# The first input tile loaded as two partition halves on two queues, and one output tile stored whole

## The chip, the cores and the metric

The kernel runs on one core of a Trainium2 chip. The metric is the device time of one execution in microseconds. The core has engines with instruction queues of their own: TensorE (PE in the profile, with its weight loads as PEld), VectorE (DVE), ScalarE (ACT), GpSimd (POOL) and SyncE (SP). In this kernel SP and ACT issue transfers between memory and the on-chip buffers, each on a queue of its own (SPq and ACTq in the profile), and POOL issues three tiny ones. Sixteen DMA engines carry them all.

## The reference

A block over 2048 tokens of width 448. Its input x is normalised per token; the result xn goes through a state-space layer and through a gated layer, and both are multiplied and added to x:

```python
xn = _layernorm(x, axis=-1)
s = _A_ref(xn, A_Lambda_re, A_Lambda_im, A_B_re, A_B_im, A_C_re, A_C_im, A_log_dt, A_Dskip)
g = _silu(_B_ref(xn, B_w_gate, B_w_up, B_w_down))
return x + s * g
```

The state-space layer is a projection of xn to 448 complex numbers, a recurrence over the tokens, and a projection back:

```python
Bu = jnp.einsum("bld,pd->blp", x + 0j, B_bar)
for t in range(L):
    h = Lam_bar[None, :] * h + Bu[:, t, :]
    hs.append(h)
y = 2.0 * jnp.einsum("blp,dp->bld", hseq, Cmat).real + x * Dskip[None, None, :]
```

The gated layer is `(sigmoid(xn @ w_gate) * (xn @ w_up)) @ w_down`, with 1792 inner columns.

## The kernel before

The tokens are 16 tiles of 128 rows, and four tiles make a chunk of 512 tokens. Tile t lies in `x_all[:, t, :]` with one token per partition. Chunk by chunk the kernel transposes the normalised tiles into `xnT`, multiplies with the gate and up weights `wG` and `wU` (14 blocks of 128 columns per chunk, `gu_mm`, L796 and L797: two 64-row matmuls side by side), projects with B (`b_phase`, L870 to L887), runs the recurrence on VectorE as two real scans in rotated coordinates (`ssm_pair`, `ssm_stack`), and forms the down projection (L1012) and the projection with C (L1041). The last steps of an output tile are on VectorE (L1050 to L1057), and SP stores it from one of three buffers `o_t` (L1061).

The order of the work on each engine is not written out by hand. Every operation is recorded with its engine, an estimated cost, and the keys that it reads and writes. A planner (`Plan.solve`) gives each one a latest start from the needs of TensorE, whose order is fixed, then simulates the engines with these estimates, and `emit` writes the instructions in the order of the simulated starts. The estimate of a transfer goes by its queue, its bytes and a rate, or by a given landing time (`land`). Transfers of SP and ACT take eight completion semaphores in turn; a transfer waits until the one eight places before it has landed. A changed transfer at the head therefore moves the semaphores of all that follow, and can change the order elsewhere.

At the head, what matters is this. SP and ACT first issue the four x tiles of chunk 0 (`load_x`, which calls `load`; the transfer is L357), tile 0 and tile 2 on SP, tile 1 and tile 3 on ACT. Behind them come the first two column blocks of `wG`, one half on each queue and each in two parts (`load_w0`), and then, on SP alone, the rest of `wG`, `wU`, four more x tiles and the row `dbc`, and the transposing loads of B (`b_load`, buffer `bT`, L394). TensorE first runs ten matmuls on constants (`warm_mm`, L443). VectorE computes the statistics of tile 0 (`bn`, L449, and `aggr`, L455), ACT the root (`root`, L483), VectorE the reciprocal (L480) and the normalised tile (`norm`, L516). TensorE transposes it (`pe_transpose`, L555 and L557), ACT copies the result out (L565), and the first gate matmuls run tile by tile (`last_tile`, L814 and L815). The statistics of tile 1 stand on VectorE between those of tile 0 and the norm of tile 0. The part of the B projection that comes first (L873) needs copies that POOL makes from `bT` (L735 and L741).

At the end, `yout` makes one output tile. Which rows one store takes is in `rows`: the tiles of the third chunk (`c == 2`) are stored as two halves of 64 rows, the others whole.

Of the kernel before, what the change touches and what calls it, by code (L numbers as in the profile page):

```python
# [14 lines left out]
ACT = mybir.ActivationFunctionType  # L15
# [3 lines left out]
D = 448  # L19
F = 1792  # L20
P = 128
H = 64
# [28 lines left out]
def dve2(n):  # L51
    return 0.067 + n / 1920.0


def dve1(n):
    return 0.067 + n / 960.0
# [17 lines left out]
class Plan:  # L74
# [10 lines left out]
    def add(self, eng, cost, fn, r=(), w=(), dma=0, lat=None, chain=False, name="", rate=230e3):  # L85
        o = Op()
        o.idx, o.eng, o.cost, o.fn, o.dma, o.name = len(self.ops), eng, cost, fn, dma, name
        o.lat = LAT.get(eng, 0.0) if lat is None else lat
        o.pre, o.suc, o.rate = {}, [], rate
        o.slot, o.land = None, 0.0  # L90
        if dma and eng != "POOL":
            o.slot, self.n_dma = self.n_dma, self.n_dma + 1
        o.start = o.end = None
        for k in r:
            if k in self.w:
                self._edge(self.w[k], o, True)
        for k in w:
            for q in self.r.get(k, ()):
                self._edge(q, o, False)
            if k in self.w:  # L100
                self._edge(self.w[k], o, True)
        for k in w:
            self.w[k] = o
            self.r[k] = []
        for k in r:
            if k not in w:
                self.r.setdefault(k, []).append(o)
        if chain or eng == "PE" or (eng in ("DVE", "ACT") and self.seq):
            key = ("chain", eng)
            if key in self.last_of:  # L110
                self._edge(self.last_of[key], o, None)
            self.last_of[key] = o
        self.ops.append(o)
        return o
# [132 lines left out]
def kernel(  # L247
# [22 lines left out]
    x_src = A_x.rearrange("b (n p) d -> p (b n) d", p=P)  # L270

    def sbt(name, shape, dt=BF16):
        return sb.tile([P] + list(shape), dt, name=name)
# [9 lines left out]
    x_all = sbt("x_all", [NT, D])  # L283
# [67 lines left out]
    add = pl.add  # L351
# [3 lines left out]
    def load(eng, key, nbytes, o, i, cost=0.45, r=(), rate=230e3, land=0.0):  # L355
        e = {"SP": Q, "ACT": A, "POOL": G}[eng]
        add(eng, cost, lambda: e.dma_start(out=o, in_=i), w=[key] if not isinstance(key, list) else key,  # L357
            r=r, dma=nbytes, chain=True, rate=rate).land = land

    def load_x(t0, n, q="SP", r=(), rate=230e3, land=0.0):  # L360
        load(q, [("x", t) for t in range(t0, t0 + n)], n * P * D * 2,
             x_all[:, t0:t0 + n, :], x_src[:, t0:t0 + n, :], r=r, rate=rate, land=land)
# [37 lines left out]

    def load_p(eng, k, r=()):
        load(eng, ("vrow", k), D * 2, vrow[k:k + 1, 0:D], (A_log_dt, A_Lambda_im, A_Lambda_re)[k].unsqueeze(0), cost=0.75, r=r)
    load_x(0, 1, "SP")
    load_x(1, 1, "ACT")
    load_x(2, 1, "SP", rate=180e3)
    load_x(3, 1, "ACT", rate=180e3)
    add("ACT", 0.05, lambda: A.preload_act_table_set("sqrt_and_others"), w=["sqrttab"], lat=1.3, chain=True)
    load_w0("SP", 0, "A", land=5.7)
    load_w0("ACT", 1, "A", land=5.9)
# [127 lines left out]
    def next_acc():  # L537
        a = acc_n[0] % 2
        acc_n[0] += 1
        return a  # L540
# [482 lines left out]
    def yout(c, j, first=False, banks=None, parts=((0, D),)):  # L1023
        js = slice(j * P, j * P + P)
        t = c * TPC + j
        g = gt_of[c, j]
        o = o_n[0] % NO
        o_n[0] += 1
        q = t % NXD
        xq = xd[q][:]  # L1030
        for pi, (c0, c1) in enumerate(parts):
            key, y = banks[pi] if banks else (lambda a: (("acc", a), acc[a][:, 0:D]))(next_acc())
            y = y[:, 0:c1 - c0]

            on_pe = len(parts) > 1 and pi == len(parts) - 1

            def f(y=y, c0=c0, c1=c1, on_pe=on_pe):
                if on_pe:
                    T.matmul(y, lhsT=ident[:, :], rhs=xq[:, c0:c1], start=True, stop=False)
                for i, (hm, cm) in enumerate(K_ORDER):  # L1040
                    T.matmul(y, lhsT=hT[c % 2][:, hm, js], rhs=cT[:, cm, c0:c1],  # L1041
                             start=(i == 0 and not on_pe), stop=(i == 6))
            n = c1 - c0
            add("PE", (8 if on_pe else 7) * (0.004 + n / 2400.0) + (SW if first else 0), f,
                r=cTk + [("hT", c % 2, p) for p in range(4)] + ([("xd", q), "ident"] if on_pe else []),
                w=[key], name=f"y{c}.{j}")
            ok = ("o", o, pi)
            od = o_t[o][:, c0:c1]
            if on_pe:
                add("DVE", dve1(n), lambda od=od, y=y, c0=c0, c1=c1: V.tensor_tensor(out=od, in0=y, in1=g_t[g][:, c0:c1], op=ALU.mult),  # L1050
                    r=[key, ("gt", g)], w=[ok])
            else:
                add("DVE", dve1(n), lambda od=od, y=y, c0=c0, c1=c1: V.tensor_tensor(out=od, in0=y, in1=xq[:, c0:c1], op=ALU.add),  # L1053
                    r=[key, ("xd", q)], w=[ok])
                add("DVE", dve2(n), lambda od=od, c0=c0, c1=c1: V.tensor_tensor(out=od, in0=od, in1=g_t[g][:, c0:c1], op=ALU.mult),
                    r=[ok, ("gt", g)], w=[ok])
            add("DVE", dve2(n), lambda od=od, c0=c0, c1=c1: V.tensor_tensor(out=od, in0=od, in1=x_all[:, t, c0:c1], op=ALU.add),  # L1057
                r=[ok, ("x", t)], w=[ok])
            rows = (0, H, P) if c == 2 else (0, P)
            for r0, r1 in zip(rows, rows[1:]):  # L1060
                add("SP", 0.45, lambda od=od, c0=c0, c1=c1, r0=r0, r1=r1: Q.dma_start(  # L1061
                    out=out_flat[t * P + r0:t * P + r1, c0:c1], in_=od[r0:r1, :]),
                    r=[ok], w=[("store", t, pi, r0)], dma=n * 2 * (r1 - r0))
# [104 lines left out]
    for c in (2, 3):  # L1168
        def mid(banks, c=c):
            for j in range(4):  # L1170
                down(c - 1, j, bank=banks[j])
                yout(c - 2, j)
        for i in range(0, 4):
            gu_step(c, i)
        b_phase(c, mid)
        if c == 2:
            prepare(3)
        for i in range(4, 14):
            gu_step(c, i)
        whole(c)  # L1180

    yout(2, 0, True)
    yout(2, 1)
    free_banks = []
    for s in range(3):
# [50 lines left out]
```

## Time and profile before

| | |
|---|---|
| median of 3 runs | 183.61 us (183.5 to 183.76) |
| profiled execution | 183.83 us, span 182.1 us |
| TensorE busy | 177.9 us of the span |
| VectorE busy | 166.4 us |
| ScalarE busy | 97.0 us |
| GpSimd busy | 40.7 us |
| x tiles of chunk 0, 112 KB each, issue to landing | SP 2.6 us, ACT 2.8 us (medians of two) |
| whole stores of 128 rows, 112 KB, issue to landing | 1.7 us, median of 11 |
| stores of 64 rows, 56 KB, issue to landing | 2.0 us, median of 8 |

The span runs from the first to the last instruction; the profiled execution's own time holds 1.73 us more around it. A row of the timeline gives start and length in microseconds, the engine, the line of the kernel, the operation, its output and inputs, and in brackets the idle time before it and what ended that. Rows of SPq and ACTq are the issuing of transfers by those queues, not the transfers. Matmul ends in the profile are modelled, so the distance between starts is what tells the pace of TensorE. A row of waits gives who waited for whom, the sum, how often, and the longest.

### The profile page before, as it was taken

To read this page: it belongs to the slowest core of one execution; us is meant where nothing else is said; L and a number is where in the kernel's file an instruction comes from. 1 tells how busy PE (TensorE), PEld (TensorE's weight loads), DVE (VectorE), ACT (ScalarE), POOL (GpSimd) and SP (SyncE) were. 2 spreads that over 40 slices of the span, in tenths; PEclk is the share of its full clock that TensorE was granted. 3 is DMA by queue.
4 is the path that set the end of the run, shared out by engine and by line. 5 is a ranking of instruction groups with operands and counts; after the bars stand their busy time and mean duration, and the time that the engine had idled before them with its cause. 6 is when DMAs were issued, how large, how long until landed. Compare 5 with 4: busy or idle time off the path is not lost.

```text
span 182.1 us, 3611 instructions
## 1 busy us (share of the span) xinstructions
PE 177.9 (98%) x1404; PEld 88.4 (49%) x1404; DVE 166.4 (91%) x296; ACT 97.0 (53%) x158; POOL 40.7 (22%) x96
## 2 busy tenths in 40 slices
PE   8999999999999999999999999999999999999992
PEld 2764444564554444445554444444555444455551
DVE  2917999999999999999999999999999999999773
ACT  3699997958899983364145543348110533411100
POOL 7183546700038997000004100000000000000000
PEclk9999999999999999999999999999999999999999
DMA  4999999999100390000004900001000000002221
GB/s 130 251 216 214 203 148 166 265 235 235 51 0 0 72 133 0 0 4 0 0 2 82 148 0 0 4 0 65 10 4 0 25 27 29 0 0 63 58 74 39
DMA packets 30003, 13.44 MB, mean 74 GB/s; under 512 B 19489, under 2 KB 29985, under 8 KB 29985
## 3 DMA queue, kind: packets, MB, share of 16 engines
q1 hardware_dynamic: 29120, 12.74, 34.4%
q10 hardware_dynamic: 768, 0.46, 0.8%
q8 instruction: 11, 0.18, 0.4%
q14 instruction: 8, 0.06, 0.1%
q0 software_dynamic: 96, 0.00, 0.0%
HBM read 6.77 MB, written 1.84 MB: 47 GB/s over the span
## 4 chain that ended last, share of the span: by engine, by line
PE 97%; DVE 1%; issue 0%; DVEq 0%
PE gu L796 43%; PE gu L1012 15%; PE acc L1041 11%; PE acc L1012 9%; PE gu L884 9%; PE gu L443 2%; PE gu L814 2%; PE acc L887 2%; PE gu L870 2%; PE acc L796 1%; PE gu L797 1%; PE acc L555 0%; PE acc L873 0%; PE gu L555 0%; DVE o_t L1057 0%; DVE o_t L1053 0%
## 5 line engine op out<-in xcount | busy, mean ns | idle before, releaser
L796 PE MATMUL gu<-xnT,wU 64*128 64x512 bf16 x196 | 45.8, 376 | 0.0
L797 PE MATMUL gu<-xnT,wU 64*128 64x512 bf16 x196 | 45.8, 376 | 0.0
L796 PE MATMUL gu<-xnT,wG 64*128 64x512 bf16 (+1 forms) x189 | 41.3, 360 | 0.0
L797 PE MATMUL gu<-xnT,wG 64*128 64x512 bf16 (+1 forms) x189 | 41.3, 360 | 0.0
L830 ACT ACTIVATE sig<-gu 128x1024 f32<-128x1024 f32 x21 | 21.4, 1022 | 25.8 <-PE gu L797 21.0
L1012 PEld LDWEIGHTS <-hF 128*128 128x128 bf16 x224 | 21.9, 98 | 20.6
L796 PEld LDWEIGHTS <-wU 64*128 64x128 bf16 x196 | 18.4, 94 | 22.9
L796 PEld LDWEIGHTS <-wG 64*128 64x128 bf16 x196 | 18.4, 94 | 19.9
L1012 PE MATMUL gu<-wd,hF 128*128 128x448 bf16 x140 | 28.0, 352 | 0.0
L833 DVE SCALAR_TENSOR_TENSOR hF<-sig,gu 128x1024 bf16<-128x1024 f32 x21 | 25.3, 1205 | 0.5 <-PE gu L797 0.3
L951 DVE TENSOR_TENSOR_SCAN wv<-c_r,st,z 128x512 bf16<-128x512 f32 x18 | 22.8, 1270 | 0.0
L1041 PE MATMUL acc<-cT,hT 128*128 128x448 bf16 (+1 forms) x112 | 22.6, 346 | 0.0
L1018 ACT ACTIVATE g_t<-gu 128x448 bf16<-128x448 f32 x10 | 5.4, 539 | 27.7 <-PE gu L1012 16.8
L797 PEld LDWEIGHTS <-wU 64*128 64x128 bf16 x196 | 18.4, 94 | 0.0
L797 PEld LDWEIGHTS <-wG 64*128 64x128 bf16 x196 | 18.4, 94 | 0.0
L1012 PE MATMUL acc<-wd,hF 128*128 128x448 bf16 x84 | 16.9, 352 | 0.0
L884 PE MATMUL gu<-xnT,bT 128*128 128x512 bf16 x72 | 16.7, 379 | 0.0
L1041 PEld LDWEIGHTS <-hT 128*128 128x128 bf16 x119 | 11.5, 98 | 10.1 <-issue 0.4
L898 ACT CAST bus<-gu 128x1024 bf16<-128x1024 f32 x12 | 12.0, 1010 | 5.8 <-PE gu L870 5.3
L527 POOL COPY xn<-xn 128x448 bf16<-128x448 bf16 x12 | 8.0, 675 | 29.9 <-ACT xn L521 29.8
L449 DVE BATCH_NORM_STATS2 bst<-x_all 128x6 f32<-128x448 bf16 x12 | 7.0, 611 | 7.7 <-DMA x_all<-in_A_x_dram 7.7
L1053 DVE TENSOR_TENSOR o_t<-acc,xd 128x448 bf16<-128x448 f32 (+1 forms) x16 | 9.5, 597 | 2.7 <-PE acc L1041 2.6
(156 smaller groups left out, 265.6 us busy)
## 6 DMA issues: line engine op xcount, KB each, us to landing
wd<-in_B_w_down_dram SPq DMA_DIRECT2D x2, 784.0 KB, 6.3
out_dram<-o_t SPq DMA_DIRECT2D x11, 112.0 KB, 1.7
wU<-in_B_w_up_dram SPq DMA_DIRECT2D x2, 448.0 KB, 11.2
x_all<-in_A_x_dram SPq DMA_DIRECT2D x2, 448.0 KB, 4.6
wG<-in_B_w_gate_dram SPq DMA_DIRECT2D x2, 336.0 KB, 7.3
wU<-in_B_w_up_dram SPq DMA_DIRECT2D x2, 336.0 KB, 9.4
wG<-in_B_w_gate_dram SPq DMA_DIRECT2D x2, 224.0 KB, 5.6
x_all<-in_A_x_dram SPq DMA_DIRECT2D x2, 224.0 KB, 9.1
```

Source lines behind the costliest of these rows:

```text
L449: add("DVE", 0.56 if t < TPC else 0.6, lambda: V.bn_stats(out=bst[b][:], in_=x_all[:, t, :]), r=[("x", t)] + ([("xnT", 0, 3, "a")] if 3 < ...
L527: add("POOL", 0.25 if n == H else 0.6, lambda: G.tensor_copy(out=o[:, D:D + n], in_=o[:, 0:n]), r=[("xn", b)], w=[("xnw", b)])
L796: T.matmul(bank[0][:, ts], lhsT=w_[0:H, s, ms], rhs=x[0:H, SL[s], ts], start=(s == 0), stop=(s == 6))
L797: T.matmul(bank[1][:, ts], lhsT=w_[H:P, (s + 1) % 7, ms], rhs=x[H:P, SL[s], ts], start=(s == 0), stop=(s == 6))
L830: add("ACT", act(1024), lambda: A.activation(th, gu[a][:], ACT.Tanh, scale=0.5), r=[("gu", a)], w=[tk])
L833: add("DVE", dve1(1024), lambda: V.scalar_tensor_tensor(out=ho, in0=th, scalar=1.0, in1=gu[a][:], op0=ALU.add, op1=ALU.mult), r=[("gu", a) ...
L884: T.matmul(gu[slots[pt]][:, i, :], lhsT=bT[:, kt, i, pt * P:pt * P + P], rhs=x[:, kt, :], start=(first and kt == 0), stop=(not first and k ...
L898: add("ACT", act(1024), lambda: A.copy(out=bus[u][:], in_=gu[slots[pt]][:]), r=key(pt), w=[("bus", u)])
L951: dve(1.194, lambda k=k: V.tensor_tensor_scan(out=wv[:, k, :], data0=rb, data1=z[:, k, :], initial=(st[pt][:, k, :] if c else 0.0), op0=AL ...
L1012: T.matmul(d, lhsT=hF[c % 2][:, m, h, js], rhs=wd[:, ft, :], start=(ft == 0), stop=(ft == FT - 1))
L1041: T.matmul(y, lhsT=hT[c % 2][:, hm, js], rhs=cT[:, cm, c0:c1], start=(i == 0 and not on_pe), stop=(i == 6))
L1053: add("DVE", dve1(n), lambda od=od, y=y, c0=c0, c1=c1: V.tensor_tensor(out=od, in0=y, in1=xq[:, c0:c1], op=ALU.add), r=[key, ("xd", q)], w ...
```

## The change

Tile 0 is loaded as two transfers of 64 partitions, the lower half on SP and the upper half on ACT. An operation without an engine joins both into the key `("x", 0)` that the statistics read. Tile 1 moves from ACT to SP, behind the lower half; tile 2 moves from SP to ACT, behind the upper half; tile 3 moves from ACT to SP, behind tile 1. SP thus issues three x transfers and ACT two. In the stores, the first tile of the third chunk (`j == 0`) is stored whole and the other three as halves, so the number of transfers that take semaphores is the same at the end as before.

```diff
-    load_x(0, 1, "SP")
-    load_x(1, 1, "ACT")
-    load_x(2, 1, "SP", rate=180e3)
-    load_x(3, 1, "ACT", rate=180e3)
+    for h, eng in enumerate(("SP", "ACT")):
+        ps = slice(h * H, h * H + H)
+        load(eng, ("x0", h), H * D * 2, x_all[ps, 0, :], x_src[ps, 0, :])
+    add("NONE", 0.0, lambda: None, r=[("x0", 0), ("x0", 1)], w=[("x", 0)], lat=0.0)
+    load_x(1, 1, "SP")
+    load_x(2, 1, "ACT", rate=180e3)
+    load_x(3, 1, "SP", rate=180e3)
...
-            rows = (0, H, P) if c == 2 else (0, P)
+            rows = (0, H, P) if c == 2 and j else (0, P)
```

The changed kernel has three lines more at its head, so a line number below that is higher by 3 in its profile (L449 becomes L452). In the instruction lists the order on TensorE is the same. On ACT, one evacuation of a gate block (L827) stands ahead of the norm of tile 4 (L521) instead of behind two norms, and one cosine table (L673) ahead of two norms; on POOL a copy of `bT` (L735) stands ahead of the copy of tile 6 (L527) instead of behind it; on VectorE three instructions change places with neighbours. The fourth `load_w0` transfer, on ACT, gets a wait for the semaphore of the lower half of tile 0.

## The prediction

> **What bounds the kernel now.** I read the page first: the share of TensorE, the chain that ended last, and the transfers.
>
> ```profile
> span 182.1 us, 3611 instructions
> PE 177.9 (98%) x1404; PEld 88.4 (49%) x1404; DVE 166.4 (91%) x296; ACT 97.0 (53%) x158; POOL 40.7 (22%) x96
> PE 97%; DVE 1%; issue 0%; DVEq 0%
> out_dram<-o_t SPq DMA_DIRECT2D x8, 56.0 KB, 2.0
> x_all<-in_A_x_dram SPq DMA_DIRECT2D x2, 112.0 KB, 2.6
> ```
>
> TensorE is the whole chain. A change to loads can only count where TensorE waits. I therefore took the list of waits for the whole span next. Only the first three of these rows stop TensorE or feed what stops it.
>
> ```profile
> POOL bT L741 <- DMA bT<-in_A_B_im_dram: 1.0, 1, 1.0
> PEld L555 <- DVE g_t L516: 0.9, 1, 0.9
> PEld L873 <- POOL bT L741: 0.5, 2, 0.3
> ```
>
> There are two places. The first is the start. The timeline of the first microseconds shows it (start, length, instruction):
>
> ```profile
> 0.72 0.87 SPq L357 DMA_DIRECT2D x_all<-in_A_x_dram  x2
> 0.73 0.90 ACTq L357 DMA_DIRECT2D x_all<-in_A_x_dram  x2
> 1.64 4.66 SPq L357 DMA_DIRECT2D wG<-in_B_w_gate_dram  x6
> 1.69 1.61 ACTq L357 DMA_DIRECT2D wG<-in_B_w_gate_dram  x2
> 3.26 0.63 DVE L449 BATCH_NORM_STATS2 bst<-x_all 128x6 f32<-128x448 bf16 x1 [3.26 <-DMA x_all<-in_A_x_dram]
> 4.03 0.59 DVE L449 BATCH_NORM_STATS2 bst<-x_all 128x6 f32<-128x448 bf16 x1
> 4.75 0.38 DVE L516 TENSOR_SCALAR g_t<-x_all,mvf,rsd 128x448 bf16<-128x448 bf16 x1
> 5.19 0.82 PE L555 MATMUL acc<-ident,g_t 128*128 128x128 bf16 x6
> ```
>
> Tile 0 lands at 3.24, its statistics start at once, the normalised tile is ready at 5.13, and the first transposes start at 5.19. The ten warming matmuls are spaced 0.427 us and the last starts at 4.56, so TensorE would be free at 4.99. It loses only 0.20 us to tile 0.
>
> The second place is the first projection with B, at 29 us:
>
> ```profile
> 28.65 0.53 POOL L741 COPY bT<-bT 64x64 bf16<-64x64 bf16 x2 [1.02 <-DMA bT<-in_A_B_im_dram]
> 28.94 0.09 PEld L873 LDWEIGHTS <-bT 64*128 64x128 bf16 x1 [0.32 <-POOL bT L741]
> 29.23 0.09 PEld L873 LDWEIGHTS <-bT 64*128 64x128 bf16 x1 [0.20 <-POOL bT L741]
> ```
>
> Here TensorE waits some 0.27 us for two POOL copies of the last bT transfer, which lands at 28.54. That transfer is the end of one line of transfers that SP issues without a pause from 3.68 us (x, wG, wU, dbc, bT). So two chains meet at 29.2: TensorE's own work, with 0.27 us to spare, and the line of SP's transfers, with nothing to spare. Behind that place TensorE starts every matmul where the one before it ends, apart from a constant 0.09 us at each change between 64-row and 128-row tiles. The table of stretches shows how full the transfers are (the last two columns are DMA share and GB/s):
>
> ```profile
> 2.20:3.40 1.20, 1.20 (x5) 0.42 (x3) 0.14 (x1) 0.74 (x1) 1.12 (x4) 1.00 0.98 334
> 3.40:4.40 1.00, 1.00 (x4) 0.34 (x3) 0.97 (x3) 0.19 (x1) 1.00 (x8) 1.00 0.50 121
> 4.40:5.40 1.00, 1.00 (x5) 0.21 (x4) 0.90 (x6) 0.40 (x2) 0.31 (x4) 1.00 1.03 298
> ```
>
> From 4.4 us the DMA engines are full, and stay so until 22; in 3.4 to 4.4 they are half idle while the first wG blocks start. What is lost there comes out at 29.2.
>
> **The change, part by part.** All is summed against the profiled execution, 183.83 us (span 182.1 and 1.73 around it); the median of the runs shown is 183.61, 0.22 less.
>
> *Tile 0 in halves.* Half the rows per queue means half the packets ahead of the last one. In the trace the sixteen completion packets of tile 0 lie between 2.56 and 2.91, and each of a DMA engine's packets takes 0.041 us. Eight packets of tile 1 run between those of tile 0; without them it ends 8 x 0.041 = 0.33 us earlier. Against it stands the issue. No 64-row load of x is in the trace, but 64-row stores are: eight of them took 0.47 to 0.70 us to issue (mean 0.57) where a 128-row store takes 0.33 to 0.40, and landed 2.0 us after issue where a whole one takes 1.7. So tile 0 lands between 0.33 us earlier and, if the stores' 0.3 us comes whole on top of today's 2.51 us with no packets saved, 0.3 us later. I take the sum of the two effects, 0.33 less 0.2, about 0.1 us earlier. The Trainium skill (DMA: Bandwidth & Descriptors, Anatomy of one DMA) fits 2.0 us plus bytes over 436 GB/s, for the gpsimd path; by it, as an estimate, halving 112 KB saves 0.13 us. The 56 KB stores of this trace contradict the sign, and they are what I go by; with the fit alone the sum would be the no-change case below.
>
> *What an earlier tile 0 is worth.* Statistics, root, reciprocal and norm all follow by the same 0.1 us. Tile 1 moves behind the half on SP: issue at about 0.73 + 0.57 + 0.05 = 1.35, and at tile 2's present 2.59 us to landing it is there at 3.9 instead of 3.41. Its statistics start at 4.03 now, so this is just hidden; its cover is the 0.6 us of tile 0's statistics. TensorE then starts 0.1 us earlier (at most 0.2). Until 6.6 us it runs at half pace (a transpose takes 0.11 us in the chain at 6.01 and 0.06 at 8.30), so this is worth 0.05 to 0.1 us of later work. At 29.2 it is worth nothing, because the bT transfer still lands when it does: 0.
>
> *SP's line.* SP issues three x transfers instead of two before wG: 0.73, plus 0.57, 0.42, 0.42 and 0.05 between them, so wG's first block is issued at 2.29 instead of 1.64 and the second at 3.08 instead of 2.43, ending at 3.69. The third block is issued at 3.68 now, held back by a POOL memset that ends at 3.66 and by tile 1's landing; this 0.64 us of waiting takes up the extra issue almost whole. So from the third block on SP is late by 0 to 0.2 us (0.70 us for the half). On the engines, 64 more rows of x are on SP's queue and 64 fewer on ACT's, and SP's wG packets start up to 0.6 us later in just the half-empty stretch. Before 4.0 us that queue moved only some 27 KB of wG; at 298 GB/s it costs 0.09 us to make up. If the whole ramp shifts by 0.6 us and nothing fills in, 0.6 x 170 GB/s = 100 KB, or 0.33 us. Lower end: ACT's queue, 64 rows lighter, fills the gap, and the line is up to 0.1 us early. I take 0.15 us, nearer the row of what was moved then. It reaches 28.54 unshortened, since SP pauses nowhere, and then TensorE: +0.15 us.
>
> *The new wait on ACT.* Transfers take eight completion semaphores in turn. With one more, the ninth is the second wG block on ACT, which now waits for tile 0's lower half. It is issued at 2.45 now (0.86 us) and lands at 6.89; it would be issued at about 3.2. Behind it on ACT is only the first root at 4.21; ACT is free at 4.06, so this is hidden by 0.15 us. On its queue the block stands behind the first block, whose packets run past 4.6, so most of the 0.75 us is hidden too; TensorE needs it at 7.06. Between 0 and 0.75 - 0.17 = 0.58 us of wait there, of which the 0.27 us at 29.2 takes up all but 0.31. I take 0.
>
> *The store.* Two SP issues (0.56 and 0.59 us) and two transfers become one of some 0.33 us, around 165 us. SP is idle around it and its o_t buffer is needed again three tiles later; TensorE does not wait there: 0. Were the cover gone, it could cost nothing, as it is less work.
>
> *What the planner moves.* The orders on TensorE are the same. ACT evacuates one gate block (0.54 us) ahead of the norm of tile 4, POOL copies bT (0.35 us, after the landing at 24.9) ahead of tile 6's copy (now at 24.07), and on DVE three instructions change places with neighbours. The work that hides them: chunk 1's transposed tiles land at 29.3 to 33.0 and TensorE needs the first at 34.75. A shift of tile 6 by 1.3 us stays inside it. 0.
>
> Sum: 0 + 0.15 + 0 + 0 + 0 = +0.15: 183.98 for the profiled execution, 183.76 against the median; I say 183.8.
>
> **The rivals.**
> 1. *No change, the bT wait hides all.* If the SP line is back on time by the third block (it waits 0.64 us before it now), the start's gain is swallowed at 29.2 and the time stays: 183.6. For it: SP's slack just equals the extra issue. Against: the half-empty engines at 3.4 to 4.4.
> 2. *Faster.* Place: the meeting at 29.2. ACT's lighter queue brings its wG forward, the half-idle stretch is filled better, and the transfer line is early; then TensorE can win up to the 0.27 us that it waits there, no more without a gain at the start as well: 183.61 - 0.27 = 183.34. It decides as soon as bT lands before 28.54. Against: ACT now waits for a landing, and SP has more rows.
> 3. *Slower through SP.* The half costs its whole issue, 0.57 + 0.05 us, because the line is limited by the queue and not by SP's issue: 183.61 + 0.62 = 184.23.
> 4. *Slower through ACT.* The wG block comes 0.75 us late, TensorE stands at 7.06: +0.31, 183.9.
> 5. *The clock.* TensorE's half pace lasts longer than 6.6 us. Each microsecond costs half a microsecond, so 0.74 us later costs 0.37: 184.0 and up. The runs before differ by 0.26 us in all, so this has hardly moved. The Trainium skill (TensorE: Matmul & The Clock Gate, Part 1) says that the window which decides is free-running; no run here shows its phase, and the granted clock reads 1.00 in this stretch although the spacing is double.
>
> **How the numbers follow.** Forecast (0 to +0.35) 0.50; no change 0.20; faster 0.14; through SP 0.09; through ACT 0.05; the clock 0.02. About 0.2%, 0.37 us, is what a measurement can tell from no change. Slower by more: case 3, half of what passes the forecast's upper end (0.04), a part of 4, and 5: 0.17. Faster by more needs both the 0.27 us and the start: 0.07. Within: 0.76. The likeliest case alone spans 183.6 to 183.95; the range takes in most of 2 and half of 3, so 183.35 to 184.2.
>
> **What would show it.** Right: tile 0's statistics start between 3.1 and 3.3, the half loads take 0.45 to 0.7 us to issue, the first transposes start between 5.0 and 5.2, the last bT transfer lands 0.05 to 0.35 us after 28.54, and the wait of L873's counterpart for POOL grows while the rest of TensorE's starts keep their distances. Wrong: bT landing before 28.5 (case 2), a new wait of the 64x128 matmuls on wG at 7 us (case 4), or half pace beyond 7 us (case 5).

## The result and the profile after

The changed kernel takes 184.31 us (median of 16 runs, 183.81 to 184.67). The kernel before takes 183.49 us in the runs beside it (16 runs, 183.33 to 184.48). The ratio is 1.0038, with a 95% interval of 1.0028 to 1.0048. On the 183.61 us that were shown at the start, this is 0.70 us slower (0.51 to 0.88). The forecast was 0.15 us slower, with a range of 183.35 to 184.2: the median lies 0.11 us above the upper end, and its interval (184.12 to 184.49) reaches into the range. A second measurement, told below, gave 1.0033 (1.0018 to 1.0047).

The profiled execution of the changed kernel took 184.67 us (span 182.9), which is the longest of its sixteen. Its waits may therefore be larger than those of a usual execution, and the sizes below go by the medians where both are to be had. Where two values are set side by side, as in 3.12 after 3.26, the first belongs to the kernel in question and the second to the kernel before.

Three lines of the page after: the span, the engines' busy time, and the chain that ended last.

```profile
span 182.9 us, 3605 instructions
PE 177.2 (97%) x1397; PEld 87.8 (48%) x1404; DVE 166.4 (91%) x296; ACT 96.9 (53%) x158; POOL 38.7 (21%) x96
PE 83%; DVE 5%; ACT 4%; DMA 3%; issue 1%; SPq 1%; POOL 1%; DVEq 0%; ACTq 0%
```

TensorE's busy time has not grown (177.2 after 177.9, with seven of 1404 matmuls missing from the records), but the span has, by 0.8 us. The chain was 97% TensorE before; now it also runs through transfers (3%) and VectorE (5%). TensorE waits for others. The waits between 2 and 32 us after say for whom (who waits for whom, sum, times, longest):

```profile
PEld L817 <- DMA wG<-in_B_w_gate_dram: 1.1, 2, 0.7
DVE rsd L502 <- POOL sdb L500: 1.1, 1, 1.1
PE gu L817 <- DMA wG<-in_B_w_gate_dram: 0.8, 2, 0.5
```

None of the three was among the waits before, and the wait for POOL's copies of `bT` is missing. The first microseconds after, as a timeline (start, length, engine, line):

```profile
0.72 1.68 SPq L357 DMA_DIRECT2D x_all<-in_A_x_dram  x3
0.73 1.48 ACTq L357 DMA_DIRECT2D x_all<-in_A_x_dram  x2
2.27 1.47 ACTq L357 DMA_DIRECT2D wG<-in_B_w_gate_dram  x2
2.45 4.25 SPq L357 DMA_DIRECT2D wG<-in_B_w_gate_dram  x6
...
3.12 0.63 DVE L452 BATCH_NORM_STATS2 bst<-x_all 128x6 f32<-128x448 bf16 x1 [3.12 <-DMA x_all<-in_A_x_dram]
4.12 0.63 DVE L452 BATCH_NORM_STATS2 bst<-x_all 128x6 f32<-128x448 bf16 x1 [0.15 <-DMA x_all<-in_A_x_dram]
5.30 0.51 PE L558 MATMUL acc<-ident,g_t 128*128 128x128 bf16 x6
...
7.09 0.23 PE L817 MATMUL gu<-xnT,wG 64*128 64x128 bf16 x1 [0.54 <-DMA wG<-in_B_w_gate_dram]
...
7.83 0.23 PE L817 MATMUL gu<-xnT,wG 64*128 64x128 bf16 x1 [0.23 <-DMA wG<-in_B_w_gate_dram]
```

- Tile 0's statistics start 0.14 us earlier (3.12 after 3.26). Tile 1 lands at 4.09, 0.15 us after VectorE is ready for it, and so the gain is gone: the first transposes start at 5.30 after 5.19.
- SP issues `wG` at 2.45 instead of 1.64, ACT at 2.27 instead of 1.69.
- TensorE stands twice at the first gate matmuls. The first stop ends when SP's first block lands (7.04; it was 5.90). The second ends when SP's second block lands (7.78; it was 6.68). Tile 2's transposes follow at 8.72 after 7.96. **At the head of this execution, 0.76 us are lost.**

What the transfers do meanwhile is seen in the stretches (start and end, length, busy times of the engines; the last two columns are DMA share and GB/s):

```profile
2.20:3.40 1.20, 1.20 (x4) 0.42 (x3) 0.28 (x1) 1.16 (x1) 1.12 (x4) 1.00 0.91 216
3.40:4.40 1.00, 1.00 (x4) 0.32 (x3) 0.81 (x3) 0.42 (x2) 1.00 (x8) 1.00 0.99 293
4.40:5.40 1.00, 0.86 (x4) 0.10 (x3) 0.92 (x5) 0.30 (x1) 0.18 (x4) 1.00 0.82 192
```

In 2.2 to 3.4 the engines move 216 GB/s where they moved 334, which is 142 KB less. The next stretch, half idle before, makes this up (293 after 121). But what it carries is still mostly x, and `wG` comes behind: tiles 1, 2 and 3 land at 4.09, 4.50 and 5.06, where all four tiles had landed by 4.01. In 4.4 to 5.4 the engines move 192 GB/s where they moved 298, so nothing is made up for `wG`.

At 29 us, TensorE and its weight loads after:

```profile
29.71 0.27 PE L876 MATMUL acc<-xnT,bT 64*128 64x256 bf16 x2
29.82 0.92 PE L873 MATMUL gu<-xnT,bT 64*128 64x512 bf16 x4
...
30.35 0.09 PEld L873 LDWEIGHTS <-bT 64*128 64x128 bf16 x1 [0.43 <-issue]
...
30.67 0.50 PE L890 MATMUL acc<-xnT,bT 128*128 128x256 bf16 x3
```

The two 64x256 matmuls, which before stood 0.27 us for POOL, run without a pause: `bT` landed at 27.27, TensorE came 0.76 us later. This gives 0.27 us back. Then TensorE stops again at 30.04, for 0.31 us. The row names no releaser ("issue"). VectorE's reading of a gate bank (L836; the kernel lets TensorE write a bank of matmul results again only when they have been read) ends at 30.29, just before TensorE goes on, so this bank is taken to be what it waits for; in a kernel below the profile names it. The end of this stretch, L890, is 0.79 us late (30.67 after 29.88), and the span ends 0.8 us late. VectorE is late because it was blocked at 22 us, here after:

```profile
22.45 0.73 POOL L500 TENSOR_TENSOR sdb<-veb,halfc 128x2 bf16<-128x2 bf16 x1
23.21 0.17 DVE L502 RECIPROCAL rsd<-sdb 128x2 f32<-128x2 bf16 x1 [1.10 <-POOL sdb L500]
```

and the same reciprocal before, which waited for nothing:

```profile
21.96 0.17 DVE L499 RECIPROCAL rsd<-sdb 128x2 f32<-128x2 bf16 x1
```

POOL's `sdb` for tiles 6 and 7 stands on POOL behind the copy of tile 5, and that copy waits for ACT's norm. On ACT the planner has put the evacuation L830 (L827 before) ahead of the norm of tile 4. The norms come later, then POOL, then VectorE. The cause is argued here from one pair of traces; the experiments with the order test it.

### The profile page after: what moved, and what is told of

Its sections match the earlier page's. It is cut to its first block, busy times and chain, and to the rows that moved or that the text cites. A ratio compares the mean times of both kernels' runs of the same rounds, so it can differ in the third digit from the quotient of the medians.

```text
span 182.9 us, 3605 instructions
## 1 busy us (share of the span) xinstructions
PE 177.2 (97%) x1397; PEld 87.8 (48%) x1404; DVE 166.4 (91%) x296; ACT 96.9 (53%) x158; POOL 38.7 (21%) x96
## 4 chain that ended last, share of the span: by engine, by line
PE 83%; DVE 5%; ACT 4%; DMA 3%; issue 1%; SPq 1%; POOL 1%; DVEq 0%; ACTq 0%
PE gu L799 34%; PE gu L1015 14%; PE acc L1044 11%; PE acc L1015 9%; PE gu L887 8%; ACT hF L833 3%; DVE hF L836 3%; DMA wG<-in_B_w_gate_dram 3%; PE acc L890 2%; PE gu L873 2%; PE gu L817 2%; ACT hT L658 1%; SPq L357 1%; DVE hT L669 1%; PE gu L800 1%
## 5 line engine op out<-in xcount | busy, mean ns | idle before, releaser
L836 DVE SCALAR_TENSOR_TENSOR hF<-sig,gu 128x1024 bf16<-128x1024 f32 x21 | 25.3, 1204 | 0.5 <-PE gu L800 0.3
L887 PE MATMUL gu<-xnT,bT 128*128 128x512 bf16 x65 | 15.3, 379 | 0.4
L530 POOL COPY xn<-xn 128x448 bf16<-128x448 bf16 x12 | 7.5, 627 | 29.8 <-ACT xn L524 29.5
L452 DVE BATCH_NORM_STATS2 bst<-x_all 128x6 f32<-128x448 bf16 x12 | 7.0, 614 | 6.6 <-DMA x_all<-in_A_x_dram 6.6
```

Of the source, the lines that this page charges most:

```text
L452: add("DVE", 0.56 if t < TPC else 0.6, lambda: V.bn_stats(out=bst[b][:], in_=x_all[:, t, :]), r=[("x", t)] + ([("xnT", 0, 3, "a")] if 3 < ...
L530: add("POOL", 0.25 if n == H else 0.6, lambda: G.tensor_copy(out=o[:, D:D + n], in_=o[:, 0:n]), r=[("xn", b)], w=[("xnw", b)])
L836: add("DVE", dve1(1024), lambda: V.scalar_tensor_tensor(out=ho, in0=th, scalar=1.0, in1=gu[a][:], op0=ALU.add, op1=ALU.mult), r=[("gu", a) ...
L887: T.matmul(gu[slots[pt]][:, i, :], lhsT=bT[:, kt, i, pt * P:pt * P + P], rhs=x[:, kt, :], start=(first and kt == 0), stop=(not first and k ...
```

## The experiments

Each kernel was timed against the kernel before on the same chip. The first four shared one chip (before 183.79 us), the next four another (183.78 us), and the last two ran on the first again (183.78 us). Single executions of one kernel spread over 0.5 to 1.7 us, so a trace shows where a wait is, and the ratio with its interval shows what a part costs.

### The head alone, without the new store

```diff
-            rows = (0, H, P) if c == 2 and j else (0, P)
+            rows = (0, H, P) if c == 2 else (0, P)
```

> The head of the changed kernel, with the third chunk's first tile stored in halves as before. Two theories. W: the time is lost because SP issues its first two wG blocks later (2.46 and 3.17 us instead of 1.64 and 2.43), so that they land after TensorE is ready for them; the store has no part in it: +0.5 to +0.9 us against before, the same as the changed kernel. S: a part of the loss is the store and the places of the completion semaphores at the end: less than +0.4 us.

Measured: 184.97 us, ratio 1.0057 (1.0035 to 1.0079). The loss is there without the store. TensorE waits 0.56 us for SP's second `wG` block (landed at 7.68). The interval overlaps that of the whole change. The median is 0.59 us above the one that the change had on this chip (184.38, below), more than the store by itself accounts for (also below); why is not known.

### Tile 3 on SP, no halves

```diff
-    load_x(3, 1, "ACT", rate=180e3)
+    load_x(3, 1, "SP", rate=180e3)
```

(on the kernel before)

> No halves: before, with tile 3 alone moved from ACT to SP, behind tile 2. W: SP's first wG block is issued at about 2.1 us instead of 1.64, TensorE waits for it, and the kernel is 0.2 to 0.6 us slower than before. H, the rival by which the halves themselves cost the time (issue of 64 rows, later tile 1, a normalised tile 0 that is 0.1 us late): tile 0 and tile 1 are loaded as before, so within 0.1 us of before.

Measured: 184.0 us, ratio 0.9997 (0.9979 to 1.0016). SP issues `wG` at 2.11 and its blocks land at 6.65 and 7.38. TensorE waits 0.40 and 0.39 us for them and transposes tile 2 at 8.31, 0.35 late. But at 29 it has no wait for POOL, and L887 starts at 29.94 after 29.88. A delay of this size at the head is hidden by the wait at 29. The time is H's, though the waits are W's. A third x transfer on SP is thus not enough to explain the loss.

### Tile 3 behind the first `wG` blocks of SP

```diff
-    load_x(3, 1, "SP", rate=180e3)
...
     load_w0("ACT", 1, "B", land=6.9)
+    load_x(3, 1, "SP", rate=180e3)
```

(on the changed kernel)

> The changed kernel with tile 3 on SP behind the first two wG blocks instead of ahead of them. W: SP's first wG blocks are issued at about 2.0 and 2.65 us, land 0.4 to 0.5 us earlier than in the changed kernel, and the wait of the first gate matmuls goes down by as much: +0.1 to +0.4 us against before. H: the halves are all there, so it stays at +0.6 to +0.8 us.

Measured: 184.54 us, ratio 1.0027 (1.0008 to 1.0047), which is 0.50 us, between the two ranges that were expected. SP's blocks are early now, 5.28 and 6.40, earlier even than before. Now ACT's second block is the late one (7.58), and tile 3 itself (7.32):

```profile
7.62 0.09 PEld L818 LDWEIGHTS <-wG 64*128 64x128 bf16 x1 [0.94 <-DMA wG<-in_B_w_gate_dram]
...
8.72 0.17 PEld L578 LDWEIGHTS <-g_t 128*128 128x128 bf16 x3 [0.32 <-DVE g_t L519]
```

A column block needs all four parts of `wG`, and the wait has moved from SP's part to ACT's. Tile 2 is transposed at 8.73, as in the change. The theory that SP's line alone makes the delay is wrong. This kernel has an order of its own on ACT, POOL and VectorE, neither that of before nor that of the change, so its time does not tell of the loads alone.

### Tile 3 left on ACT

```diff
-    load_x(3, 1, "SP", rate=180e3)
+    load_x(3, 1, "ACT", rate=180e3)
```

(on the changed kernel)

> The changed kernel with tile 3 left on ACT, behind tile 2. W in its narrow form (only SP's blocks count): SP's wG at about 2.0 us, +0.1 to +0.4 us against before. W in a wider form (either queue's wG, whichever has more x ahead of it): ACT's first wG blocks are then issued at about 2.7 and 3.4 us, and TensorE waits for those instead: +0.4 to +0.8 us. H: +0.6 to +0.8 us with the wait of the gate matmuls where it is in the changed kernel.

Measured: 184.93 us, ratio 1.0058 (1.0035 to 1.0081). The same once more: SP's blocks land at 5.87 and 6.23, ACT's second one at 7.90, and TensorE waits 0.95 us for it. SP issues only tile 1 behind its half, and the kernel is no faster than the change. So it is not the number of x transfers on SP. What the slow kernels so far have in common is the halves and, but for the one with tile 3 behind `wG`, the moved order.

### The loads of the change, the instruction order of before

The planner is given the four x operations of before; only what they issue is exchanged. The store is that of the change.

```diff
...
+    xl = lambda eng, t, p0=0, p1=P: eng.dma_start(out=x_all[p0:p1, t, :], in_=x_src[p0:p1, t, :])
+    for t, (q, fn) in enumerate((("SP", lambda: (xl(Q, 0, 0, H), xl(A, 0, H))), ("ACT", lambda: xl(Q, 1)),
+                                 ("SP", lambda: xl(A, 2)), ("ACT", lambda: xl(Q, 3)))):
+        add(q, 0.45, fn, w=[("x", t)], dma=P * D * 2, chain=True, rate=230e3 if t < 2 else 180e3).land = 0.0
```

(on the changed kernel, in place of its own x operations)

> This kernel issues exactly the loads and stores of the change, but the planner is given the four x operations of before, so that on ACT, POOL and VectorE the instructions stand in the order of before (the norm of tile 4 ahead of the evacuation of the gate block, tile 6's copy ahead of the copy of bT). Theory: two separate losses. The late first blocks of wG cost 0.77 us at 7 us; 0.27 us of that come back at 29 us, where TensorE no longer waits for POOL's copies of bT; and the moved order costs 0.3 us at 30.35, where TensorE waits for VectorE. Without the moved order: the wait on wG at 7 us is there as in the change (tile 2's transposes at 8.6 to 8.8 instead of 7.96), no wait at 30.35, L887 at 30.3 to 30.4 instead of 29.88: time before +0.4 to +0.5. Rival, the order is harmless and all comes from the head: +0.7 to +0.8, with a wait of 0.3 us on VectorE still there, only because TensorE's evacuations are later. Rival, the order is everything: +-0.1.

Measured: 184.21 us, ratio 1.0024 (1.0007 to 1.004), which is 0.44 us (0.13 to 0.74). This is what the loads and the store cost without the moved order, and it is the time that the theory gave. The profiled execution was the fastest of its twelve (183.86) and shows only the small end of it: a wait of 0.28 us for `wG`, and VectorE's reciprocal without a wait.

```profile
7.30 0.09 PEld L815 LDWEIGHTS <-wG 64*128 64x128 bf16 x1 [0.28 <-DMA wG<-in_B_w_gate_dram]
...
22.30 0.17 DVE L499 RECIPROCAL rsd<-sdb 128x2 f32<-128x2 bf16 x1
```

Here the last of the four `wG` parts was ACT's second (7.26), which was issued only at 3.44, right after ACT's half of tile 0 had landed (3.42). The tile 2 transposes start at 8.19 and L887 at 29.89, not in the ranges that were expected, 8.6 to 8.8 and 30.3 to 30.4. The 0.44 us of the median are not seen in this trace.

### The order of the change, the loads of before

The reverse: the planner gets the five operations of the change, and they issue the four whole tiles as before. The store is that of the change here too.

```diff
...
+    [add(q, 0.45, fn, w=[("x0", h)], dma=H * D * 2, chain=True, rate=230e3) for h, (q, fn) in enumerate((("SP", xl(Q, 0)), ("ACT", xl(A, 1))))]
+    add("NONE", 0.0, lambda: None, r=[("x0", 0), ("x0", 1)], w=[("x", 0)], lat=0.0)
+    [add(q, 0.45, fn, w=[("x", t)], dma=P * D * 2, chain=True, rate=rate) for t, q, fn, rate in ((1, "SP", xl(Q, 2), 230e3), (2, "ACT", xl(A, 3), 180e3), (3, "SP", lambda: None, 180e3))]
```

(on the changed kernel, in place of its own x operations)

> The other way round: the four x loads are issued as before (whole, tile 0 and 2 on SP, 1 and 3 on ACT), but the planner is given the five operations of the change, so that ACT, POOL and VectorE have the order of the change; the store is that of the change too. The first blocks of wG should land as before and TensorE should transpose tile 2 at 7.96. Theory, with VectorE's release of the gate bank at a time that the head does not move (it was 30.33, 30.34 and 30.35 in three kernels with the moved order, at heads between +0.65 and +0.87): TensorE waits for it up to 0.8 us, L887 at 30.68, and the time is +0.6 to +0.8, so that in the change itself most of the head's loss would be covered by this one. Theory, with the release following TensorE's head: 0.3 us of wait, +0.3. Rival, the order is harmless by itself: +-0.1, no wait at 30.

Measured: 184.01 us, ratio 1.0011 (0.9993 to 1.0028), which is 0.20 us, with an interval of -0.13 to 0.51 that does not exclude 0. `wG` is on time and tile 2 is transposed at 7.84. The wait of VectorE and that of TensorE behind it are there without any change in the loads:

```profile
22.34 0.17 DVE L499 RECIPROCAL rsd<-sdb 128x2 f32<-128x2 bf16 x1 [0.88 <-POOL sdb L497]
...
29.56 0.39 PE L870 MATMUL gu<-xnT,bT 64*128 64x512 bf16 x2 [0.23 <-DVE hF L833]
```

So the wait needs only the planner's order. Its cost is less sure: L887 starts at 29.88, as before, where the kernel before loses as much to POOL's copies of `bT`. Against the kernel with the store alone, below, which transposes tile 2 at the same time (7.82) and waits for neither, L887 is 0.43 us late. All five executions with that order have TensorE's wait for the bank (0.40 us here; 0.31, 0.13, 0.33 and 0.10 us in the change, the head alone, tile 3 on ACT and the change again), and none of the seven others has it. One of these seven, the next kernel, has the change's order on POOL but not on ACT: its reciprocal waits 0.23 us and TensorE not at all for the bank, and VectorE has read the bank by 29.07, as in the kernel with the store alone (29.06), where it was 29.50 here. So the move on POOL by itself does not make the wait. VectorE's own wait for POOL is less sharp a mark: 0.43 to 1.11 us with the moved order, but also up to 0.62 without. The expectation that VectorE's release stays at 30.35 whatever the head does was wrong: it moves with the head, and the expectation of about 0.3 us was the better one.

### The row `dbc` behind the transposing loads of B

```diff
-    load("SP", "dbc", P * D * 2, dbc[:], A_Dskip.unsqueeze(0).to_broadcast((P, D)), rate=400e3, land=22.7)
...
+    load("SP", "dbc", P * D * 2, dbc[:], A_Dskip.unsqueeze(0).to_broadcast((P, D)), rate=400e3, land=29.0)
```

(on the kernel before; the new place is behind the four loads of B)

> Before, with the load of the row dbc moved behind the transposing loads of B on SP's queue, so that bT lands earlier. It measures what the wait at 29 us is worth by itself. Theory: bT lands 0.5 to 1.3 us earlier, TensorE has no wait for POOL's copies at 29, L887 at 29.6 instead of 29.88, time -0.25 to -0.3. Rival: something else is next within 0.27 us (VectorE, the gate bank at 30, since POOL's copies change places here too): 0 or slower, up to +0.5.

Measured: 183.66 us, ratio 0.9995 (0.9975 to 1.0015). It tells nothing of the wait at 29, because it did not move it: the last B transfer landed at 28.39 after 28.54, POOL copied at 28.50, and TensorE waited as before.

### The store alone

```diff
-            rows = (0, H, P) if c == 2 else (0, P)
+            rows = (0, H, P) if c == 2 and j else (0, P)
```

(on the kernel before)

> Before, with the third chunk's first tile stored whole and nothing else. Theory and rival agree on 0 (within 0.15 us): the order of the other engines is that of before but for two neighbours on VectorE, and TensorE waits nowhere near 165 us. More than 0.2 us either way would mean that the store is part of the change's loss.

Measured: 183.62 us, ratio 0.9994 (0.9977 to 1.0011), which is -0.11 us (-0.42 to 0.20). No cost of the store is seen. By chance this run also shows what the wait at 29 is worth. Its `bT` landed at 27.58, so TensorE did not wait, and from L873 to L887 it took 0.64 us (28.81 to 29.45) where before took 0.93 (28.95 to 29.88): 0.29 us.

### The change again, and tiles 2 and 3 in one transfer

> The change once more, on the same chip as the next kernel and in a second profiled execution. The first profiled execution took 184.67 us, the longest of its sixteen; this one should be nearer the median. Theory: +0.6 to +0.8 on the median as measured first (1.0028 to 1.0048), a wait of 0.3 to 0.9 us for wG at 7 us again, and again VectorE blocked by POOL's square-root input for about 1 us at 22 to 23 us. If the first trace was an odd one, one of the two waits is missing and the loss is under 0.4.

Measured: 184.38 us, ratio 1.0033 (1.0018 to 1.0047). The profiled execution took 184.08 us, the shortest of its twelve. It shows the same two waits, smaller at the gate matmuls and hardly felt by TensorE at 30:

```profile
7.30 0.09 PEld L817 LDWEIGHTS <-wG 64*128 64x128 bf16 x1 [0.45 <-DMA wG<-in_B_w_gate_dram]
...
22.69 0.17 DVE L502 RECIPROCAL rsd<-sdb 128x2 f32<-128x2 bf16 x1 [0.99 <-POOL sdb L500]
```

SP's second block (7.26) is the last one again; ACT's second came at 6.75. The last kernel takes the loads of the change with the order of before, and joins tiles 2 and 3 into one transfer on ACT:

```diff
...
-                                 ("SP", lambda: xl(A, 2)), ("ACT", lambda: xl(Q, 3)))):
+                                 ("SP", lambda: xl(A, 2, 2)), ("ACT", lambda: None))):
```

(on the kernel with the order kept; `xl` now takes the number of tiles as well)

> Tile 0 in halves as in the change, the instruction order of before and the store of the change, but tiles 2 and 3 as one transfer of 224 KB on ACT behind the upper half, so that each queue issues only two x transfers ahead of wG. The head then has eight transfers and none waits for another one's landing. Theory, what makes wG late is the number of issues ahead of it: SP issues wG at about 1.98 and 2.65 (in the change 2.46 and 3.17), ACT at about 2.25 and 2.95 with no wait for a landing; the four parts are there by 7.1, the wait at 7 us is under 0.15 and the time is +-0.2 of before. Rival, what makes wG late is the rows of x ahead of it on a queue (320 on ACT here, as many as SP has in the change): the parts on ACT land at 7.3 or later, TensorE waits 0.3 or more, and the time is +0.4 or more, as with the order kept alone.

Measured: 184.34 us, ratio 1.0024 (1.0007 to 1.0041), as with the order kept alone. The issues came as planned (SP 1.98 and 2.69, ACT 2.27 and 2.95, no wait for a landing), and yet SP's second block landed at 8.00 and ACT's at 7.82:

```profile
8.04 0.09 PEld L814 LDWEIGHTS <-wG 64*128 64x128 bf16 x1 [1.11 <-DMA wG<-in_B_w_gate_dram]
```

SP's second block was issued only 0.27 us later than before and landed 1.32 us later. So the number of issues ahead of `wG` is not the cause by itself, nor is the wait of ACT. The rival, the rows of x ahead on the same queue, gets the time right and ACT's late parts, but not that SP's block, behind only 192 rows, was the last of all. What the kernels with halves share is the start. The stretch 2.2 to 3.4 us of this kernel, then of the kernel with the order alone, and of that with the store alone (last column GB/s):

```profile
2.20:3.40 1.20, 1.20 (x5) 0.41 (x3) 0.04 (x1) 1.16 (x1) 1.12 (x4) 1.00 0.95 211
```

```profile
2.20:3.40 1.20, 1.20 (x5) 0.41 (x3) 0.18 (x1) 0.74 (x1) 1.12 (x4) 1.00 1.00 331
```

```profile
2.20:3.40 1.20, 1.20 (x5) 0.41 (x3) 0.12 (x1) 0.74 (x1) 1.12 (x4) 1.00 0.99 329
```

| tile 0 | GB/s in 2.2 to 3.4 us | waits for `wG` at 7 us |
|---|---|---|
| whole, two x per queue (4 kernels) | 314 to 334 | at most 0.06 |
| whole, three x on SP (1 kernel) | 247 | 0.79 in sum |
| in halves (7 executions) | 190 to 240 | 0.28 to 1.12 in sum |

The transfers of the halves also begin later. These rows show how busy the transfer engines were (tenths, slices of 0.05 us from 1.6 to 3.6 us), in the kernel before and in the changed one:

```profile
DMA  0008999904300469999999999999999999987542
DMA  0000000000447958559786794679999969929237
```

The first packet of x starts at 1.75 to 1.77 us in the five executions with whole tiles and at 2.09 to 2.10 us in the seven with halves. After that the engines have pauses where they were full before. This goes with halves in every trace. It does not order the waits: 190 GB/s went with a wait of 0.56 us, 240 with 0.95, 215 with 0.28 and 211 with 1.11.

## Why the prediction was right or wrong

It had the sign of the likeliest case right and the size too small: 0.15 us for 0.70. The way by which the time is lost was another than the one forecast. Step by step:

**SP's line** is the step that failed, in two ways. The issue times were forecast well enough (2.29 and 3.08; measured 2.45 and 3.16; the third block is 0.32 late, forecast 0 to 0.2). But the delay was carried to the wrong place. The prediction let the line matter only through the end of `bT` at 28.54, "since SP pauses nowhere". The runs contradict that: `bT`'s last landing lay between 27.27 and 29.30 over the twelve traces, and in the changed kernel, with SP starting later, it was 1.27 us *earlier* than before. Nor were the engines full from 4.4 us on, as it read: in the kernel before their share is 0.78 and 0.89 in 5.4 to 6.4 and 6.4 to 7.4 us, at 198 and 214 GB/s. What the late start does delay is the first `wG` blocks themselves. SP's two landed at 5.90 and 6.68 before and were needed at 6.73 and 7.06. The second had 0.38 us to spare, while the step itself had it 0.65 us late at its issue. The prediction made this comparison for ACT's second block and not for SP's two. Its own upper estimate, "100 KB, or 0.33 us" if the ramp shifts and nothing fills in, was near the size of the loads' loss (0.44), but it was put down as an end of the range, and in the wrong place, so the nearness is luck.

**What the planner moves**, put at 0, is the second term that failed. By the kernel with the order alone it is 0.20 us, with an interval that includes 0; TensorE's wait for the bank is shown in each trace with that order and in no other. The prediction followed tile 6 to TensorE's transposed tiles, needed at 34.75. It did not follow the queue the other way: VectorE's reciprocal waits for POOL, and the reading of the gate banks is queued behind it on VectorE.

The kernels that gave 0.44 and 0.20 both hold the new store, which by itself measured -0.11 (-0.42 to 0.20). Counted once, the three make 0.44 + 0.20 + 0.11 = 0.75, against 0.70 and, the second time, 0.61 for the whole change. The terms cannot be parted more finely than their intervals, which leave room for an order that costs nothing.

**Tile 0 in halves**, forecast 0.1 us earlier, was right for the one trace (0.14) and wrong as a rule. In seven executions with halves the statistics start at 3.12 to 3.44, mean 3.28; in five with whole tiles at 3.22 to 3.32, mean 3.27. The halves took 0.59 us to issue, near the 0.57 taken from the 64-row stores, but the sum set only 0.2 us of this against the 0.33 that fewer packets save. The first packets started 0.33 us later, and this eats the saving whole. The Trainium skill (DMA: Bandwidth & Descriptors, Rules for kernel authors) says of two transfers to disjoint partition halves "Don't bother — they serialize", and advises one 128-partition transfer. By that rule the gain is nothing; the seven executions agree. It would have been the sentence to weigh before.

**What an earlier tile 0 is worth**: that 0.27 us at 29.2 swallow what happens at the head was right, but it worked on a loss instead of a gain. The kernel with tile 3 on SP shows it best: 0.35 late at 8.3, 0.06 late at 29.9. Tile 1's cover was too thin in the first profiled execution of the change: it landed at 4.09, not 3.9, and VectorE waited 0.15 us. In the second it landed at 3.53.

**The new wait on ACT**, put at 0 with 0 to 0.58 as its bounds, lies inside them and is not the main cause. The trace shows it as a wait for the half that ACT itself loads, the upper one, and not for the lower half, as is said above: ACT's second block is issued at 3.12, right after that half's landing at 3.10, while SP's half had landed at 2.88. In both traces of the change SP's block was the last to land. With the order kept it was ACT's, after a wait that held its issue until 3.44; but without that wait, with tiles 2 and 3 in one transfer, the time was the same.

**The store**: no cost seen, as forecast.

Of the rivals, *slower through SP* (184.23) gave nearly the time, by luck. Its mechanism, a transfer line limited by the queue up to 29, is not what the runs show: `bT` did not land later in the changed kernel's first trace, and 0.13 us later in its second. *Slower through ACT* had the place right, a wait at 7 us, and named the wrong queue. `bT` landing before 28.5 was to be the sign of a faster kernel; the first trace has it and is slower. *The clock* is not the loss: the transposes ran at full pace from 5.3 us in the changed kernel's first trace, and at half pace until 6.6 before.

What stays open: how the weaker start becomes a late `wG` block, now on SP and now on ACT, and how large the wait is in one execution. For the weaker start itself, beside the later first packet, an estimate from the rows is at hand. With halves only 112 KB are issued until 1.32 us, not 224 KB until 1.14, and 112 KB at the 319 GB/s that the kernel before moved from 2.2 to 3.0 us last 0.36 us, while the next tile on each queue is issued 0.64 us after the first. This was argued from the rows and not tested by itself. No kernel that was tried is faster than the one before by more than its interval.

## What to carry to other kernels

When something is put ahead of a load, compare that load's landing with the moment it is needed, for every part of it and on every queue; a line of transfers is not rigid, and its far end may arrive earlier although its start is later. Splitting a first tile over two queues does not bring it sooner if each half takes longer to issue than the whole and its packets start later. And when a planner moves an instruction on a side engine, follow who waits for that engine in both directions, since its queue can hold up a second engine and, through it, the bank that the busiest one needs.

## What was not expected of the hardware

- A 64-row load of 56 KB occupies its queue longer than a 128-row load of 112 KB: 0.58 to 0.60 us against 0.40 to 0.41, in all traces. The whole tile behind the half took another 0.85 us on ACT and 0.56 on SP, where the second whole tile took 0.45 and 0.42 before.
- A stretch in which the transfer engines count as busy can carry very different amounts: in 2.2 to 3.4 us a share of 0.95 went with 211 GB/s with halves, and 1.00 with 331 with whole tiles. The DMA share alone does not tell that a stretch is well used.
- TensorE's change to full pace came by 5.3 us in some executions and between 6.0 and 6.7 us in others, also where the loads were the same: before, the transposes of tile 0 were 0.107 us apart, in the kernel with the store alone 0.056. The granted clock read 1.00 in both. That the window which decides runs freely, as the Trainium skill has it (TensorE: Matmul & The Clock Gate, Part 1), fits this. With the loads of before, the first gate matmul started at 6.36 us with the early change and at 6.59 to 6.73 with the late one. By the transposes of tile 2 this was lost again in the kernel with the store alone (7.82, against 7.83 in the kernel with `dbc` moved).
